# Cosine attention and a gated feed-forward layer on one core: the hand-written opening order replaced by another one

## Chip, cores, metric

One NeuronCore of a Trainium2 chip runs the kernel. The metric is the device time of one execution in microseconds (us). The engines are TensorE (PE, with its weight loads as PEld), VectorE (DVE), ScalarE (ACT), GpSimd (POOL) and SyncE (SP), which only issues DMAs here.

## What is computed

```
# q, k, v: (8 batches, 12 heads, 448 positions, 64); tau = 0.1
q_n = q / (norm(q, axis=-1) + 1e-6);  k_n = k / (norm(k, axis=-1) + 1e-6)
attn = softmax(q_n @ k_n.T / tau)                  # over 448 keys
x = (attn @ v) with heads side by side             # (3584, 768)
h = x @ w_in                                       # w_in (768, 2048)
out = (h * clip(h + 3, 0, 6) / 6) @ w_out          # w_out (2048, 768), float32
```

## The kernel before

**Work.** The heads are taken two at a time, 48 pairs in all and six to a batch. An "item" j is the q or the k of two pairs (448 KB); items 2d and 2d+1 belong to pairs 2d and 2d+1. When the six pairs of a batch are done, the batch's x stands transposed in `xT`, and the feed-forward layer runs on it in "units": 16 units of the first matrix product per batch (`mm1_unit`, line 589: six matmuls of 448 columns, line 598), and units of the second product, most of them by a fast two-by-two scheme with sums of weight blocks and of g blocks (`product_unit`, line 794, eight matmuls of 384 columns; `mm2_unit`, line 659, 16 of them). The first unit of batch 1 is the 17th.

**Order.** Nothing is reordered by a scheduler (`tc.manual_schedule()`): each engine runs its instructions in program order and waits on semaphores. The program has two parts. `PLAN` is a list of strings; each word is a step that `run` and `do` execute, so that PLAN writes out the order of everything from the first load to the turn of pair 17. After it a loop over pairs 18 to 47 places the same steps by rule, one pair a turn, with the feed-forward units of `TURNS` in between. All DMAs of inputs and outputs and all transposing DMAs are issued by SP, one after another, and weights by POOL.

The words, with the engine where it is fixed (otherwise a letter says it: a ScalarE, v VectorE, p POOL) and the line of the profile:

- `LQ.j` loads item j (SP, line 198), `LV.d` the v of two pairs (SP, four DMAs, line 212), `W` the next weight piece (POOL, line 1004; cast to bf16 on the way).
- `SQ.j.e.c.n` squares n of the columns of item j (lines 227 and 229), `RE.j` sums the squares over the head size (VectorE, line 241; `RE.j.h` one half). `NO.d` makes the reciprocal norms of two items with four ScalarE instructions (lines 257 to 260); `NA.d` (lines 272, 273) and `ND.d` (lines 284, 285) do the same with two on ScalarE and two on VectorE. `NM.j` multiplies (line 297; with a last number, one half).
- `TR.j` transposes item j on PE (line 342), or `XD.j` by a transposing DMA (SP, line 353). `CQ`, `CK`, `CS` copy the result to where the scores read it (lines 362, 364, 392, 402).
- `SC.i.g` are the scores of pair i, group g (PE, line 445), `EX.i.g` their exponentials (ScalarE, line 463), `VA.i.g` the products with v (PE, line 486), `FI.i` the division by the row sums (VectorE, lines 506, 507), `VC.i` the cast of v.
- `BK` and `CX` transpose a pair's result on PE and copy it into `xT`; `XP` and `XB` do it by DMA (lines 550, 538).
- `U` issues the next feed-forward unit on PE, `UA`, `UV` and `UP` the oldest open step on its results on ScalarE (relu, line 614), VectorE (product, line 620, which frees the PSUM bank) and POOL. `WS` sums weight blocks, `GS` blocks of g. `WS.y3` and `WS.y4` write over blocks of w_out that `mm2_unit` reads, so they follow units 31 and 32.
- `D.n` and `DP.n` are matmuls of zeros that keep PE busy while it has nothing to do (512 columns, line 1011; 248 columns, line 1016).

Until `OPEN`, scores go to two double PSUM buffers; after it, six single banks are handed out in a fixed ring (`next_bank`), to scores, units and transposes alike, and PE waits until the bank's last reader is done.

The weights: `w_in` comes in four pieces, two halves of its columns by two halves of its rows, and `w_out` in four pieces of four of its 16 row blocks; an assertion in `mm1_unit` holds that the pieces that a unit reads were issued:

```
assert len(weights) <= 6 - 2 * (2 * fc // FCN)
```

Of the kernel before, what the change touches and what calls it, by code (L numbers as in the profile page):

```python
# [18 lines left out]
ORDER = "1111111111111111111111111111112222222122"  # L19

PLAN = [
# [39 lines left out]
]  # L61


# [1 line left out]
def kernel(  # L65
# [11 lines left out]
    B, H, S, D = q.shape  # L77
    d_model, d_ff = moe_w_in.shape
# [5 lines left out]
    FCN = d_ff // 128  # L84
# [6 lines left out]
    w_in_r = moe_w_in.tensor.rearrange("(g n p) f -> g p n f", g=2, p=64)  # L91
# [10 lines left out]
    w_in_sb = const.tile([128, CC, d_ff], BF16, name="w_in_sb", tag="w_in_sb")  # L102
# [65 lines left out]
    def needs(*what):  # L168
        for w in what:
            assert w in issued or any(x < 0 for x in w[1:] if isinstance(x, int)), w  # L170
# [399 lines left out]
    def g_of(b):  # L570
        if b == B - 1:
            needs(("NM", NP - 1), ("RE", NP - 1), ("VC", NP - 1))
            return g_last
        return gT[b % 2]
# [15 lines left out]

    def mm1_unit(b, fc, ends=None):
        needs(*(("CX", i) for i in range(b * HP, (b + 1) * HP)))
        assert len(weights) <= 6 - 2 * (2 * fc // FCN)
        x, g, c0 = xT[b % 2], g_of(b), b % 2 * SR
        ps, key = bank_of(None, 1)
        def products_of(ccs):
# [83 lines left out]
    def firsts(b, *fcs):  # L680
        return [(mm1_unit, b, fc) for fc in fcs]
# [301 lines left out]
    f = firsts(b, *range(FCN))  # L983
# [3 lines left out]
    for n, x in enumerate("2176"):  # L987
# [4 lines left out]
    units[NP] += [(product_unit, n, x, 2) for n, x in ((10, "7"), (10, "6"), (11, "6"))]  # L992
    units[NP] += [(product_unit, 11, "7", x) for x in range(2)]

    FG = d_ff // 2
    weights = [
        (w_in_sb[64 * g : 64 * g + 64, :, f * FG : (f + 1) * FG], w_in_r[g, :, :, f * FG : (f + 1) * FG])
        for f in range(2)
        for g in range(2)
    ] + [(w_out_sb[:, 4 * f : 4 * f + 4, :], w_out_r[:, 4 * f : 4 * f + 4, :]) for f in range(4)]  # L1000

# [76 lines left out]
    SC = [psum_s.tile([128, 2, 512], FP32, name=f"SC{n}", tag=f"SC{n}") for n in range(2)]  # L1078
# [114 lines left out]
```

## Time and profile before

| | |
|---|---|
| three runs | 404.18, 404.43, 405.69 us; median 404.43 |
| the profiled execution | 402.04 us, of which the span of the program's instructions is 399.5 |
| busy, share of the span | PE 98%, VectorE 72%, ScalarE 68%, POOL 61%, weight loads 58% |
| granted TensorE clock | 1.00 in the profiled execution |
| chain that ended last | PE 90%, ScalarE 3%, VectorE 3%, POOL 2%, DMA 1% |

A row of a timeline gives start, duration, engine, source line, operation and tiles; of engines that overlap two instructions, the duration runs past the next one's start, and the distance of two starts is what an instruction costs in a full queue. The chain of waits is followed back from the last instruction, at each step to what released it. Sums by stretch give the busy time and the number of instructions of each engine between two moments.

### The profile page before, as it was taken

To read this page: it belongs to the slowest core of one execution; us is meant where nothing else is said; L and a number is where in the kernel's file an instruction comes from. 1 tells how busy PE (TensorE), PEld (TensorE's weight loads), DVE (VectorE), ACT (ScalarE), POOL (GpSimd) and SP (SyncE) were. 2 spreads that over 40 slices of the span, in tenths; PEclk is the share of its full clock that TensorE was granted. 3 is DMA by queue.
4 is the path that set the end of the run, shared out by engine and by line. 5 is a ranking of instruction groups with operands and counts; after the bars stand their busy time and mean duration, and the time that the engine had idled before them with its cause. 6 is when DMAs were issued, how large, how long until landed. Compare 5 with 4: busy or idle time off the path is not lost.

```text
span 399.5 us, 9630 instructions
## 1 busy us (share of the span) xinstructions
PE 391.9 (98%) x3677; PEld 231.6 (58%) x3677; DVE 289.5 (72%) x513; ACT 271.9 (68%) x624; POOL 242.6 (61%) x236
## 2 busy tenths in 40 slices
PE   7999999999999999999999999999999999999996
PEld 4666555555665556555555555555565556555564
DVE  6897689899877598776778775886766565645663
ACT  6899988776977676887776776767658655224230
POOL 7899556392654999389859829688395500400070
PEclk9999999999999999999999999999999999999999
DMA  8999977999988677795778397895853424230133
GB/s 292 299 229 260 235 186 147 243 165 211 175 175 187 157 203 176 177 229 154 188 187 225 79 184 183 169 180 142 187 131 70 102 48 67 46 74 21 30 71 97
DMA packets 91565, 63.73 MB, mean 160 GB/s; under 512 B 56064, under 2 KB 89984, under 8 KB 91520
## 3 DMA queue, kind: packets, MB, share of 16 engines
q1 hardware_dynamic: 87408, 56.45, 59.7%
q0 software_dynamic: 3712, 6.29, 9.1%
q8 instruction: 28, 0.46, 0.5%
q10 hardware_dynamic: 400, 0.39, 0.3%
q14 instruction: 17, 0.14, 0.1%
HBM read 45.61 MB, written 11.01 MB: 142 GB/s over the span
## 4 chain that ended last, share of the span: by engine, by line
PE 90%; ACT 3%; DVE 3%; POOL 2%; DMA 1%; issue 1%; SPq 0%; POOLq 0%; ACTq 0%
PE M L598 23%; PE M L794 18%; PE PV L486 11%; PE Y L598 6%; PE M L445 6%; PE Z L598 5%; PE Z L794 5%; PE Y L794 4%; PE PV L1016 3%; ACT at L463 2%; PE M L874 1%; PE Z L445 1%; PE Y L445 1%; DMA tT<-nrm 1%; PE SC L445 1%; PE M L659 1%
## 5 line engine op out<-in xcount | busy, mean ns | idle before, releaser
L598 PEld LDWEIGHTS <-w_in_sb 128*128 128x128 bf16 x768 | 72.1, 98 | 63.0 <-issue 2.5
L463 ACT ACTIVATE at<-M 128x448 bf16<-128x448 f32 x199 | 99.4, 574 | 13.5 <-PE M L445 12.0
L598 PE MATMUL M<-xT,w_in_sb 128*128 128x448 bf16 x510 | 107.8, 353 | 0.0
L297 POOL TENSOR_TENSOR nrm<-big,r 128x896 bf16<-128x896 f32 (+1 forms) x47 | 79.0, 1685 | 25.9 <-ACT at L463 9.5
L229 POOL TENSOR_TENSOR big<-big 128x896 f32<-128x896 f32 (+3 forms) x42 | 65.1, 1555 | 14.2 <-DVE n L241 8.7
L614 ACT ACTIVATE u<-M 128x448 bf16<-128x448 f32 x85 | 47.9, 565 | 31.0 <-PE M L598 30.0
L486 PEld LDWEIGHTS <-at 128*128 128x128 bf16 (+1 forms) x1536 | 53.8, 97 | 22.9 <-issue 13.7
L620 DVE SCALAR_TENSOR_TENSOR gT<-u,M 128x448 bf16<-128x448 bf16 x74 | 45.2, 617 | 28.5 <-ACT u L614 28.4
L486 PE MATMUL PV<-vx,at 128*128 128x65 bf16 (+1 forms) x1536 | 63.2, 193 | 0.2 <-DVE on L507 0.2
L241 DVE TENSOR_REDUCE n<-big 128x14 f32<-128x896 f32 (+1 forms) x50 | 51.8, 1041 | 5.8 <-POOL big L229 4.8
L794 PEld LDWEIGHTS <-gT 128*128 128x128 bf16 x336 | 32.5, 98 | 23.5 <-DVE gT L772 0.7
L823 POOL TENSOR_TENSOR big<-big 128x384 f32<-128x384 f32 x13 | 13.4, 1033 | 53.7 <-ACT big L842 53.5
L794 PE MATMUL M<-w_out_sb,gT 128*128 128x384 bf16 x216 | 39.0, 326 | 0.3 <-DVE gT L772 0.3
L794 PEld LDWEIGHTS <-gs 128*128 128x128 bf16 x280 | 27.0, 98 | 18.7 <-issue 0.6
L402 POOL COPY km<-tT 64x128 bf16<-64x128 bf16 x34 | 12.6, 372 | 38.1 <-DMA tT<-nrm 20.5
L507 DVE TENSOR_TENSOR on<-PV,rc 128x512 bf16<-128x512 f32 x48 | 33.2, 692 | 1.7
L794 PE MATMUL M<-w_sum,gs 128*128 128x384 bf16 (+1 forms) x192 | 34.1, 323 | 0.1
L445 PE MATMUL M<-tT,kz 64*128 64x448 bf16 (+1 forms) x177 | 31.9, 351 | 0.1
L463 ACT ACTIVATE at<-Y 128x448 bf16<-128x448 f32 x47 | 27.0, 574 | 6.1 <-PE Z L445 5.9
L598 PE MATMUL Z<-xT,w_in_sb 128*128 128x448 bf16 x132 | 28.7, 353 | 0.0
L463 ACT ACTIVATE at<-Z 128x448 bf16<-128x448 f32 x48 | 27.6, 575 | 1.2 <-PE Z L445 0.8
L598 PE MATMUL Y<-xT,w_in_sb 128*128 128x448 bf16 x126 | 27.3, 353 | 0.0
(140 smaller groups left out, 560.1 us busy)
## 6 DMA issues: line engine op xcount, KB each, us to landing
big<-in_k_dram SPq DMA_DIRECT2D x24, 448.0 KB, 4.4
big<-in_q_dram SPq DMA_DIRECT2D x24, 448.0 KB, 4.2
out_dram<-o SPq DMA_DIRECT2D x107, 96.0 KB, 2.2
big<-in_v_dram SPq DMA_DIRECT2D x48, 128.0 KB, 4.1
big<-in_v_dram SPq DMA_DIRECT2D x48, 96.0 KB, 4.0
w_in_sb<-in_moe_w_in_dram POOLq DMA_DIRECT2D x4, 768.0 KB, 11.4
w_out_sb<-in_moe_w_out_dram POOLq DMA_DIRECT2D x4, 768.0 KB, 8.7
tT<-nrm SPq DMA_TRANSPOSE x34, 2.8
```

Source lines behind the costliest of these rows:

```text
L229: engines[e].tensor_tensor(out=o, in0=i, in1=i, op=ALU.mult)
L241: nc.vector.tensor_reduce(out=n2s[d % 2][:, j % 2, c], in_=sq[:, :, :, :].rearrange("p g c d -> p (g c) d")[:, c, :], axis=AX.X, op=ALU.add,)
L297: engines[e].tensor_tensor(out=nrm[:, :, g, :].rearrange("p c g d -> p g c d"), in0=raw_of[j][:, g, :, :], in1=rs[d % 2][3][:, j % 2, :] . ...
L445: nc.tensor.matmul(o, ks, qt[rows], start=True, stop=True)
L463: nc.scalar.activation(out=o, in_=x, func=AF.Exp, scale=inv_tau)
L486: nc.tensor.matmul(pv_out(j, h), at[rows, n, q_cols(i // HP, j)], vt[rows, 3 + h if name == "M" else 5 * h + int(name[1]), :], start=(name ...
L507: nc.vector.tensor_tensor(out=on[:, :, :, :].rearrange("p j h d -> p h j d"), in0=pv4[:, :, :, 0:D], in1=rc[:, :, :].to_broadcast([128, 2, ...
L598: nc.tensor.matmul(ps[:, 0:S], w_in_sb[:, cc, fc * 128 : (fc + 1) * 128], x[:, cc, 0:S], start=(cc == 0), stop=(cc == CC - 1),)
L614: nc.scalar.activation(out=u[:, :], in_=ps[:, 0:S], func=AF.Relu, bias=0.5, scale=1.0 / 6.0)
L620: nc.vector.scalar_tensor_tensor(out=g[:, fc, c0 : c0 + S], in0=u[:, :], scalar=1.0, in1=ps[:, 0:S], op0=ALU.min, op1=ALU.mult,)
L794: nc.tensor.matmul(m, lhs[:, c, :], rhs[:, c, c0 : c0 + width], start=(base is None and c == 0), stop=(c == KC - 1), skip_group_check=True,)
L823: nc.gpsimd.tensor_tensor(out=e, in0=d, in1=e, op=ALU.add)
```

## The change

PLAN is replaced by another order of the same work. What differs beside the order:

- Fill: 92 matmuls instead of 93, with `D.10` first of all.
- The first two items are squared whole on ScalarE; before, ScalarE, POOL and VectorE shared them. Over the plan ScalarE squares 16 times (before 13, some of them parts), POOL 10 (17), VectorE 3 (4).
- Six `NA`/`ND` and six `NO` (before one and eleven).
- `NM` on VectorE for items 2, 5, 7 and 19 (before 2, 12 and 18).
- Copies: `CK` on ScalarE four times (one), `CQ` three (one), `CX` four (two), `CS` once (three times). `VC` on POOL 13 times (nine), on ScalarE two (three), on VectorE five (eight).
- `W` ten times (eight): the first half of the columns of `w_in` in quarters. Five pieces are issued before the first unit (before two).
- `WS.7.p.0` alone is on POOL; before, `WS.6.p.0` too.
- `LV.11` stands before `XP.14` and `NO.10` before `SQ.22`; before, after them.

```diff
-    "LQ.1 DP.5 SQ.1.a.11.3 SQ.1.p.4.3 DP.1 SQ.1.a.0.4 LQ.0 SQ.0.p.8.6 DP.2 DP.4 LQ.3 LQ.2 SQ.1.v.7.4 RE.1.1",
-    "SQ.0.a.0.6 RE.1.0 NO.0.1 LQ.5 LQ.4 SQ.0.v.6.2 DP.6 SQ.3.a.0.7 NM.1.p.0 D.10 RE.0.1 DP.3 NM.1.p.1 RE.0.0 DP.8",
-    "NO.0.0 LV.0 DP.2 SQ.2.a.0.7 NM.0.p.0 RE.3 RE.2 NM.0.p.1 TR.1.Y DP.2 TR.0.Z CK.0.v DP.4 SQ.4.p.0.7 CQ.0.v",
-    "SQ.5.a.0.7 LQ.6 NO.1 LV.1 LQ.7 SC.0.0.0 SC.0.1.1 DP.5 DP.3 CQ.1.v EX.0.0 RE.5 RE.4 NM.3.p SC.0.2.0 CK.1.v",
...
-    "EX.7.0 LQ.13 SC.7.1 SC.7.2 FI.5 TR.9 SC.7.3 EX.7.1 VA.6.0 BK.5 EX.7.2 CK.9.v CK.8.v VA.6.1 CX.5.v CS.9.a",
-    "VA.6.2 EX.7.3 U LQ.15 SC.8.0 UA CS.8.v VC.8.a SC.8.1 EX.8.0 U VA.6.3.h UV SC.8.2 U VC.9.v EX.8.1 W SC.8.3",
...
-    "VA.16.2 VA.16.3.h SC.17.2 SC.17.3 FI.16 EX.17.1 XP.14 LV.11 U UA U U XB.16 UV UV EX.17.2 UV EX.17.3 SQ.22.a.0.7",
-    "VA.17.0 CS.18.v NO.10 CK.19.v VC.19.v NM.20.p RE.22 VC.18.p",
+    "D.10 LQ.1 DP.7 DP.5 LQ.0 SQ.1.a.0.14 DP.8 SQ.0.a.0.14 RE.1.1 LQ.3 DP.4 RE.1.0 LQ.2 NA.0.1 RE.0.0 ND.0.1",
+    "NM.1.p.1 NM.1.p.0 SQ.3.a.0.7 RE.0.1 DP.5 NO.0.0 LQ.5 SQ.2.a.0.7 NM.0.p.0 TR.1.Y DP.8 NM.0.p.1 DP.10 TR.0.Z",
+    "RE.3 LQ.4 CK.0.v CK.1.v RE.2 CQ.0.v NO.1 SQ.5.p.0.7 LV.0 SQ.4.a.0.7 DP.8 LQ.6 SC.0.0.0 EX.0.0 SC.0.1.1",
+    "EX.0.1 CQ.1.v DP.5 DP.4 NM.3.p SC.0.2.0 TR.3.Y RE.5 VC.0.v EX.0.2 RE.4 LV.1 VA.0.0 LQ.8 SC.0.3.1 DP.3 NM.2.v",
+    "SC.1.0.0 NA.2 CK.2.v TR.2.Z LQ.7 EX.0.3 ND.2 SC.1.1.1 EX.1.0 LV.2 NM.5.v DP.9 VC.1.v SC.1.2.0 CQ.2.v CQ.3.v",
...
+    "CX.4.v EX.7.1 VA.6.0 VA.6.1 LQ.12 SQ.10.p.0.7 BK.5 EX.7.2 TR.9 RE.10 CX.5.a CS.8.v SC.7.3 U CK.8.a CS.9.a",
+    "SQ.11.p.0.7 SC.8.0 U EX.7.3 UA SQ.12.p.0.7 CK.9.a LV.4 EX.8.0 VA.6.2 UA LQ.13 VA.6.3.h RE.11 SC.8.1 UV",
...
+    "EX.14.2 VA.14.0 VA.14.1 UA SC.14.3 GS.-1.5 SC.15.0 GS.-1.2 EX.14.3 NM.18.p UV U SQ.20.a.0.7 UA WS.y3.v.0",
+    "LV.8 WS.6.v.1 VC.15.a VA.14.2 WS.1.v.1 U WS.y3.v.1 WS.y4.v.0 XP.12 U EX.15.0 SC.15.1 WS.7.v.1 UV UA",
+    "WS.y4.v.1 EX.15.1 SC.15.2 RE.20 SC.15.3 CK.16.v U EX.15.2 NM.19.v LQ.21 CK.17.v UA GS.-1.1 EX.15.3 CS.16.v",
...
+    "XP.14 U UA UV U EX.17.2 XB.16 U NO.10 UV EX.17.3 UV SQ.22.a.0.7 VA.17.0 CS.18.v VC.18.v RE.22 NM.20.p",
...
-        assert len(weights) <= 6 - 2 * (2 * fc // FCN)
+        assert len(weights) <= 8 - 2 * min(2, 4 * fc // FCN)
...
-    FG = d_ff // 2
+    PIECES = [slice(0, d_ff // 4), slice(d_ff // 4, d_ff // 2), slice(d_ff // 2, d_ff)]
     weights = [
-        (w_in_sb[64 * g : 64 * g + 64, :, f * FG : (f + 1) * FG], w_in_r[g, :, :, f * FG : (f + 1) * FG])
-        for f in range(2)
+        (w_in_sb[64 * g : 64 * g + 64, :, f], w_in_r[g, :, :, f])
+        for f in PIECES
         for g in range(2)
     ] + [(w_out_sb[:, 4 * f : 4 * f + 4, :], w_out_r[:, 4 * f : 4 * f + 4, :]) for f in range(4)]
```

The lines of the changed kernel stand one lower from the PLAN on (line 598 is 597 there).

58 rows, old and new, of the table PLAN are left out of this document.

## The prediction

> **What bounds the kernel now.** I read the page's busy shares, then the sums by stretch, the chain of waits in order of time, and each engine's timeline. Times are from the span's start (399.5 us). The first exponential starts at 12.14, the first feed-forward unit (six matmuls of line 598) at 41.11, the last instruction of the plan at 113.3.
>
> ```profile
> core 0: us, PE busy (x) PEld busy (x) DVE busy (x) ACT busy (x) POOL busy (x), PEclk, DMA share, GB/s
> 0.00:12.10 12.10, 9.56 (x65) 6.40 (x65) 8.54 (x31) 7.62 (x19) 9.50 (x24) 1.00 0.88 287
> 12.10:41.10 29.00, 28.44 (x403) 18.69 (x402) 24.48 (x53) 27.65 (x55) 27.32 (x23) 1.00 1.06 266
> 41.10:113.30 72.20, 72.16 (x717) 41.30 (x715) 61.04 (x110) 60.02 (x140) 40.16 (x37) 1.00 0.93 193
> 113.30:137.00 23.70, 23.12 (x232) 13.50 (x230) 17.54 (x28) 16.80 (x42) 16.22 (x15) 1.00 0.73 162
> 137.00:399.50 262.50, 258.59 (x2269) 151.73 (x2267) 177.87 (x293) 159.81 (x371) 149.43 (x140) 1.00 0.58 133
> ```
>
> PE's busy time overlaps itself, so I count its work by spacing: 0.189 us for each 448 columns, 0.162 for 384, 0.029 for 65 (starts of neighbours in a run). From 12.1 to 41.1 that gives 16.6 us of real work, from 41.1 to 113.3 it gives 67.6 of 72.2, from 113.3 to 137 it gives 21.6 of 23.7, after that 251.4 of 262.5. So PE sets the end from 41 on and loses 4.6 and 2.1 us in the two stretches that the change can reach. Before 41 it waits: ScalarE is busy for 27.65 of 29.0 us there, VectorE for 24.48. The clock is full throughout. The chain confirms both readings:
>
> ```profile
> 30.08 1.35 ACT at L463 x2
> 31.45 2.98 ACT at L463 x4
> ...
> 41.11 1.14 PE M L598 x6
> ...
> 121.07 1.08 DVE n L241
> 122.16 0.07 SPq L538
> 122.22 0.05 issue
> 122.28 0.58 SPq L198
> 122.85 0.05 issue
> 122.91 0.02 SPq L353
> 122.92 0.03 issue
> 122.95 4.33 DMA tT<-nrm
> ```
>
> The exponentials carry the start. In the loop's first turns (after 113.3) the chain leaves PE for SP's queue and a transposing DMA. SP's timeline says why:
>
> ```profile
> 111.72 1.55 SPq L550 DMA_TRANSPOSE xT<-on  x1
> 113.38 2.68 SPq L212 DMA_DIRECT2D big<-in_v_dram  x4
> 116.15 1.22 SPq L538 DMA_TRANSPOSE xT<-on  x1
> 117.47 3.43 SPq L647 DMA_DIRECT2D out_dram<-o  x4
> 121.00 1.23 SPq L538 DMA_TRANSPOSE xT<-on  x1
> ```
>
> Each row starts where the one before it ends: SP is a line of issues, and LV.11 (line 212) stands ahead of all that the loop needs.
>
> **The change, part by part.** The reordered loop after the plan is untouched; the program's work is the same but for two more weight DMAs, one matmul of fill less, five pairs of root operations (NA on ScalarE, ND on VectorE) in place of NO, and steps that change engine. Costs are start-to-start spacings of before's rows: exponential of two banks 0.80, of one 0.43; square on ScalarE 0.84, on POOL 1.64; sum RE 1.0; NO 0.99, NA 0.47, ND 0.57; normalise 1.65 on POOL, 1.0 on VectorE; FI 0.85; relu 0.43, product 0.53; weight sum 0.9.
>
> *To the first exponential.* Before, three engines share the squares and EX.0.0 starts at 12.14. After, LQ.1 and LQ.0 land at 4.20 and 5.41 as before (same issues). ScalarE squares them by 6.3; VectorE's four half sums end at 7.85; ND.0 ends at 7.3, so POOL's four half normalisations (0.9 each) run from 7.35 to 10.95; before, the last ended at 10.6. PE is the new wait: 29 small fill matmuls at 0.106 after the ten wide ones end at 9.7; TR.1 follows; behind it stand DP.8 and DP.10, 18 x 0.106 = 1.9 us, so TR.0 ends at 12.4; then eight more, and SC.0.0 at 13.25. ScalarE does SQ.4 in that hole. EX.0.0 at 13.65: **1.5 us late**.
>
> *From there to the first unit.* ScalarE's plan from EX.0.0 to EX.7.0 is 25.2 us before (28 exponentials of pairs 0 to 6, four NO, one square, one copy), and it took 26.5. After it is 22.7: of the four NO one stays, two become NA, one comes later, and CX.3 goes to VectorE (−2.97 + 0.94 − 0.41). VectorE's from EX.0.0 to the first unit rises from 24.6 to 25.7 (two normalisations, two ND, a CS and a CQ more; three CK, one RE and one VC fewer). POOL falls from 24.5 to 21.2. I followed the order by hand, each step starting at the latest of its engine's last step and its inputs: EX.1.0 at 17.3, EX.3.0 24.9, EX.4.0 27.7 (before 28.17), EX.5.0 31.0 (31.45), EX.6.0 34.4 (35.69; NO.5 and CX.3 stood ahead of it), EX.7.0 37.4 (38.67), CX.4 on VectorE 38.7, CX.5 on ScalarE 40.35, first unit's end 40.55 against 42.25. From the 1.7 us I take 0.25 for VA.6.2, now behind the unit, and 0.15 for waits I missed. **−1.3 us.** Bounds: −2.0 if ScalarE never waits, +1.5 if the late exponential stays late.
>
> *Weights.* Five pieces instead of two are issued before the first unit. POOL pays 0.70 each; it has 3.3 us less to do there. They leave POOL from 26.6 to 30.7; the slowest weight DMA of before took 13.2 us to land, so the quarters are there at 40. W6 (fc 8 and up) leaves near 43, its unit U9 runs at 56.8. Nothing. If quarters were as slow as halves and queued, still nothing until U5.
>
> *First to fortieth unit.* ScalarE's plan grows from 57.3 to 62.4 us, VectorE's falls from 63.7 to 62.4, POOL's from 45.8 to 44.0, and PE has 72. Followed the same way, with six PSUM banks handed out in order: ahead of before by 1.2 at U9 (work done included), 1.3 at U13, 1.2 at U21, 1.1 at U31. The extra ScalarE work (2.7 us of squares, three CK, two CQ, two CX) lies beside PE. Then VectorE has WS.y3.v.0, WS.6.v.1, WS.1.v.1, WS.y3.v.1, WS.y4.v.0, WS.7.v.1 in a row ahead of the copy that frees U32's bank for SC.15.3: 6 x 0.87 = 5.2 us from 93.3 (when U31 has read its first half), so 98.5 plus 0.5; PE asks at 99.2. Covered, just; if y3 must wait for all of U31 (94.5), SC.15.3 and U34 are 1.2 us later. Lead at the plan's end 0.95: **+0.35 us**, bounds −1.0 and +3.0.
>
> The last weight piece, W10, now follows NM.16 and goes out near 82.6; before, it left at 83.16 and landed at 90.82. U31's matmul 12 is the first to read it, at 93.8. No wait.
>
> *Entry to the loop.* LV.11 moves ahead of XP.14 and NO.10 ahead of SQ.22, so SP reaches XD.20 2.7 us sooner (that row), and POOL's km copies, which waited 5.8 us, go sooner too. Of the 2.1 us that PE loses there I take a quarter, since two sums on VectorE (line 772, to 120.9) stand there as before: **−0.5 us**, between 0 and −2.1. Once the loop is PE's, nothing more is won or lost.
>
> *Sum:* −1.3 + 0.35 − 0.5 = −1.45. The profiled execution took 402.04 us (span and 2.5 around it), so 400.6 for it. The runs' median, 404.43, is 2.4 above that execution; I carry the difference over: **403.0 us**.
>
> **One rule against the change.** VectorE's two-input normalise at 60.88 lasted 1.09 us, and POOL's, begun at 61.00, took 2.52 in place of 1.69: one held the other up.
>
> ```profile
> 61.00 2.52 POOL L297 TENSOR_TENSOR nrm<-big,r 128x896 bf16<-128x896 f32 x1 [1.50 <-DVE r L285]
> ```
>
> The Trainium skill (SBUF — State Buffer, Who interferes with whom) says that a VectorE instruction with two SBUF inputs and a GpSimd one that reads SBUF exclude each other, and that whichever issues first makes the other block fully. This row agrees with it. By that rule the sum stays as it is if NM.4 on POOL is the one held, and rises by at most POOL's 1.65 if NM.5 on VectorE is, both being released by ND.2.
>
> **Rivals.**
>
> *1. The waits at the loop's entry go altogether.* XD.20 lands by 123 and not 127.3, and the chain 121–134 (DMA, km copies, POOL's sums, line 851) dissolves: −1.3 + 0.35 − 2.1 = −3.0, **401.4 us**. For it: 17 us of that chain hang on one DMA. Against it: VectorE's 772 rows and ScalarE's fuller tail.
>
> *2. VectorE becomes the bound: slower.* Before, it executed 24.6 us of steps in 28.6, 4 idle. After, it begins its stretch at 12.75, and 24.3 us of steps lead to CX.4. My walk leaves it 1.65 idle. With 4 idle CX.4 ends at 41.05; if NM.5, released together with POOL's NM.4, is held for POOL's 1.65 as well (the row of line 297 above shows such a hold the other way round), at 42.7, and the first unit ends near 44, 1.7 late. Its row of weight sums then costs its 1.2: +1.7 − 0.25 + 0.35 + 1.2 = +3.0, **407.4 us**. It decides from about 3 us of VectorE idle time between 12.75 and CX.4. For it: VectorE was busy for 24.48 of 29.0 and gets more. Against it: half of its idle time before was waiting for exponentials that now come sooner.
>
> That the order is not what the text says is excluded: the instruction lists of both kernels show it.
>
> **How the numbers follow.** Forecast (403.0; its own range 402.4 to 404.4) 0.43, rival 1 0.32, rival 2 0.22, another way 0.03. A measurement of this kernel tells about 0.5% (2.0 us) from no change. Faster by over that: rival 1 and a little, 0.34; within: 0.43; slower: 0.23. The range reaches to rival 1 with its bound (−2.0 for the start) and most of rival 2: 400.0 to 406.8.
>
> **What would show it.** Right: EX.0.0 near 13.7 and EX.7.0 near 37.4; the first unit's end near 40.6; U31 (line 659) starting near 91.9 with VA.14 and SC.15.0 done; plan's end near 112.4; XD.20's issue before 120. Wrong: a first unit after 42; ScalarE waiting over 3 us between 14 and 37; SC.15 or line 794 waiting for VectorE's line 738; a wait of line 598 or 659 for weights.

## The result, and the profile after

The changed kernel takes 408.48 us (median of 6 runs, 406.80 to 409.56), the kernel before in the same comparison 404.31 (402.34 to 405.69): a ratio of 1.0116, 95% interval 1.0083 to 1.0150, so 3.4 to 6.1 us slower (the two medians alone would give 1.0103). Forecast were 403.0 us and no difference that a measurement can tell.

The profiled execution of the changed kernel took 409.56 us with a span of 406.8. Sums by stretch, cut at the first exponential (13.6), the first feed-forward unit (41.2), the end of the fortieth unit (119.3) and, as far behind it as before, at 143.0:

```profile
core 0: us, PE busy (x) PEld busy (x) DVE busy (x) ACT busy (x) POOL busy (x), PEclk, DMA share, GB/s
0.00:13.60 13.60, 11.12 (x84) 7.56 (x85) 8.40 (x32) 7.81 (x17) 8.83 (x23) 1.00 0.90 290
13.60:41.20 27.60, 25.13 (x372) 16.42 (x371) 25.44 (x54) 25.55 (x48) 22.66 (x20) 1.00 0.99 253
41.20:119.30 78.10, 75.71 (x729) 42.48 (x728) 61.73 (x113) 63.67 (x150) 39.00 (x39) 0.98 0.89 176
119.30:143.00 23.70, 22.00 (x215) 13.08 (x214) 16.65 (x28) 16.63 (x39) 14.25 (x13) 1.00 0.77 160
143.00:406.80 263.80, 259.60 (x2288) 152.16 (x2284) 177.99 (x294) 159.71 (x371) 149.69 (x141) 1.00 0.58 134
```

The first unit starts about where it did (41.21, before 40.95). In the stretch from there to the plan's end, which took 72.2 us before and takes 78.1, PE has gaps, and the clock's mean is 0.98. By starts of units: U1 to U40 (line 793) 76.78 us, before 71.06; U40 to the eighth unit behind it 14.13 and 14.10; from there to the end 274.6 and 273.4, a part in which the plan has no say and which took 273.4 to 275.5 in the profiles of the kernel before and of its variants. So the loss sits between U1 and U40. It is 5.7 us in these two executions, which lie further apart than the medians do; by the ratio the whole loss is some 4.7 us.

More than half of it is one place. VectorE's timeline, then POOL's, then PE's (the last column is the idle time before a row and what ended it):

```profile
85.72 4.50 DVE L737 TENSOR_TENSOR w_sum<-w_out_sb 128x1536 bf16<-128x1536 bf16 x1
90.14 0.61 DVE L619 SCALAR_TENSOR_TENSOR gT<-u,M 128x448 bf16<-128x448 bf16 x1
```

```profile
85.47 0.80 POOL L1003 DMA_DIRECT2D w_out_sb<-in_moe_w_out_dram  x1
86.30 3.10 POOL L737 TENSOR_TENSOR w_sum<-w_out_sb 128x1536 bf16<-128x1536 bf16 x1
```

```profile
88.30 0.36 PE L444 MATMUL M<-tT,kz 64*128 64x448 bf16 x1
90.80 0.35 PE L444 MATMUL M<-tT,kz 64*128 64x448 bf16 x1 [2.14 <-DVE gT L619]
91.08 2.17 PE L597 MATMUL M<-xT,w_in_sb 128*128 128x448 bf16 x6
```

The weight sum WS.1.v.0 takes 4.50 us; its like takes 0.95. It ends 0.82 us after POOL's sum WS.7.p.0 (89.40). In the order before, it stood ahead of POOL's two sums. VectorE, then POOL:

```profile
83.22 0.95 DVE L738 TENSOR_TENSOR w_sum<-w_out_sb 128x1536 bf16<-128x1536 bf16 x1
```

```profile
86.38 6.16 POOL L738 TENSOR_TENSOR w_sum<-w_out_sb 128x1536 bf16<-128x1536 bf16 x2
```

In the changed kernel the products behind WS.1.v.0 free PSUM banks late, and PE stands idle for 2.14 us. Then the six matmuls of U28 take 1.97 us, start to start, in place of 1.14. Sums by microsecond say why (the granted clock stands third from the end):

```profile
89.00:90.00 1.00, 0.00 (x0) 0.00 (x0) 1.00 (x1) 0.00 (x0) 0.40 (x1) 1.00 1.49 62
...
91.00:92.00 1.00, 1.00 (x5) 0.44 (x5) 1.00 (x2) 1.00 (x3) 0.00 (x0) 0.69 1.17 216
92.00:93.00 1.00, 1.00 (x4) 0.38 (x3) 1.00 (x3) 0.26 (x1) 0.00 (x0) 0.50 1.11 235
...
94.00:95.00 1.00, 1.00 (x14) 0.69 (x12) 1.00 (x3) 0.57 (x3) 0.00 (x0) 0.60 1.13 319
```

The start holds the same thing in small. VectorE, then POOL, at the two normalisations that ND.2 releases together:

```profile
17.04 0.33 DVE L284 RECIPROCAL r<-le 128x28 f32<-128x28 f32 x1
17.46 2.62 DVE L296 TENSOR_TENSOR nrm<-big,r 128x896 bf16<-128x896 f32 x1
```

```profile
17.45 1.69 POOL L296 TENSOR_TENSOR nrm<-big,r 128x896 bf16<-128x896 f32 x1 [2.78 <-DVE r L284]
19.08 1.47 POOL L315 CAST vx<-big 128x512 bf16<-128x512 f32 x1
```

NM.5 on VectorE stands until NM.4 on POOL is done and then takes its 1.0; POOL's next step, VC.3, stands until NM.5 is done. Such a step, which stands at the head of its queue until the other engine's operation is done, is called held below.

Where a loss is summed up below, PE's lost time is the time that its useful matmuls, counted at full clock, do not fill.

### The profile page after: what moved, and what is told of

It reads as the page before. It is cut to its first block, busy times and chain, and to the rows that moved or that the text cites. A ratio compares the mean times of both kernels' runs of the same rounds, so it can differ in the third digit from the quotient of the medians.

```text
span 406.8 us, 9610 instructions
## 1 busy us (share of the span) xinstructions
PE 393.6 (97%) x3676; PEld 231.7 (57%) x3676; DVE 290.2 (71%) x518; ACT 273.4 (67%) x619; POOL 234.4 (58%) x233
## 4 chain that ended last, share of the span: by engine, by line
PE 77%; DMA 8%; DVE 6%; ACT 3%; POOL 2%; issue 2%; SPq 1%; DVEq 0%; POOLq 0%; ACTq 0%
PE M L597 21%; PE M L793 17%; PE PV L485 9%; PE Y L597 6%; DMA big<-in_v_dram 5%; PE Z L793 4%; PE Y L793 4%; PE Z L597 4%; PE M L444 4%; DMA tT<-nrm 2%; ACT at L462 1%; PE M L658 1%; PE M L873 1%; PE PV L1015 1%; PE Z L444 1%
## 5 line engine op out<-in xcount | busy, mean ns | idle before, releaser
L597 PE MATMUL M<-xT,w_in_sb 128*128 128x448 bf16 x516 | 110.6, 355 | 0.2 <-DMA xT<-on 0.2
L597 PEld LDWEIGHTS <-w_in_sb 128*128 128x128 bf16 x768 | 72.2, 98 | 65.8 <-issue 6.4
L462 ACT ACTIVATE at<-M 128x448 bf16<-128x448 f32 x193 | 96.7, 568 | 15.4 <-PE M L444 13.0
L296 POOL TENSOR_TENSOR nrm<-big,r 128x896 bf16<-128x896 f32 (+1 forms) x46 | 75.9, 1655 | 33.6 <-DVE r L284 16.5
L485 PEld LDWEIGHTS <-at 128*128 128x128 bf16 (+1 forms) x1536 | 53.9, 97 | 24.3 <-issue 14.9
L228 POOL TENSOR_TENSOR big<-big 128x896 f32<-128x896 f32 (+1 forms) x35 | 58.9, 1686 | 7.6 <-ACT at L462 3.1
L462 ACT ACTIVATE at<-Y 128x448 bf16<-128x448 f32 x49 | 27.9, 569 | 6.3 <-PE Z L444 6.2
L462 ACT ACTIVATE at<-Z 128x448 bf16<-128x448 f32 x52 | 29.5, 567 | 0.4 <-PE M L444 0.4
L597 PE MATMUL Y<-xT,w_in_sb 128*128 128x448 bf16 x132 | 28.7, 354 | 0.0
L315 POOL CAST vx<-big 128x512 bf16<-128x512 f32 x41 | 27.6, 678 | 0.1
```

The costliest lines, as they stand in the source:

```text
L228: engines[e].tensor_tensor(out=o, in0=i, in1=i, op=ALU.mult)
L296: engines[e].tensor_tensor(out=nrm[:, :, g, :].rearrange("p c g d -> p g c d"), in0=raw_of[j][:, g, :, :], in1=rs[d % 2][3][:, j % 2, :] . ...
L315: (engines[e].copy if e == "a" else engines[e].tensor_copy)(out=o, in_=f)
L462: nc.scalar.activation(out=o, in_=x, func=AF.Exp, scale=inv_tau)
L485: nc.tensor.matmul(pv_out(j, h), at[rows, n, q_cols(i // HP, j)], vt[rows, 3 + h if name == "M" else 5 * h + int(name[1]), :], start=(name ...
L597: nc.tensor.matmul(ps[:, 0:S], w_in_sb[:, cc, fc * 128 : (fc + 1) * 128], x[:, cc, 0:S], start=(cc == 0), stop=(cc == CC - 1),)
```

## The experiments

Theory A: VectorE's and POOL's operations with two inputs in SBUF (the engines' on-chip memory, other than PSUM) shut each other out, and two such holds, at steps that were not held before, cost the time. The kernel before was timed beside each run again, at 402.9 to 403.8 us, so ratios are compared. Rivals: VectorE is too full, so that any step moved only moves the wait; weights that land late; ScalarE's squares.

**e1, NM.5 later.**

```diff
-    ... EX.1.0 LV.2 NM.5.v DP.9 VC.1.v SC.1.2.0 CQ.2.v CQ.3.v
+    ... EX.1.0 LV.2 DP.9 VC.1.v SC.1.2.0 CQ.2.v CQ.3.v NM.5.v
```

> The changed kernel with one step moved on VectorE: the normalisation NM.5 stands behind VC.1, CQ.2 and CQ.3 and not ahead of them, so that it no longer starts in the same moment as NM.4 on POOL (17.46 and 17.45 us, both released by ND.2; NM.5 took 2.62 us in place of 1.0). Theory A, the two engines exclude each other and the start-up lost 1.2 us by this one hold: NM.5 takes 1.1 us at most 1.3, the gap of 0.83 us ahead of EX.2.0 on ScalarE goes, EX.7.0 starts near 37.4 (38.62 in the changed kernel), the first unit near 40.0 (41.21), and the time falls by 1.2 us, to about 407.3. Rival R, VectorE is simply too full there: the steps behind NM.5 come sooner but others later; EX.7.0 stays after 38.3 and the time within 0.4 us of 408.5.

407.10 us, ratio 1.0089 (1.0060 to 1.0119). VectorE's timeline:

```profile
19.18 1.66 DVE L296 TENSOR_TENSOR nrm<-big,r 128x896 bf16<-128x896 f32 x1
```

Still 0.66 held (NM.4 ran from 18.21 to 19.90), but behind the copies that mattered. This execution began 0.8 later (EX.0.0 at 14.36), so distances count: from EX.0.0 to EX.7.0 23.83 us, 25.03 in the changed kernel, and 25.0 to 25.2 in every other run that left NM.5 and the start's order in place. The hold costs 1.2 us at the first unit. Theory A holds here; the time fell by 0.27%, 1.1 us, though the intervals overlap.

**e2, WS.1.v.0 later**, behind WS.6.v.0.

```diff
-    EX.13.3 CS.14.v UV UA WS.1.v.0 LV.9 ...
+    EX.13.3 CS.14.v UV UA LV.9 ...
-    ... NO.9 U UV W WS.6.v.0 VA.13.3.h
+    ... NO.9 U UV W WS.6.v.0 WS.1.v.0 VA.13.3.h
```

> The changed kernel with one step moved on VectorE: the weight sum WS.1.v.0 (85.72 us, 4.50 us long in place of 0.95) stands behind WS.6.v.0, some 4.6 us of VectorE's work later, when POOL's WS.7.p.0 (86.30 to 89.40) is over. Theory A, POOL's two-input sum held it, the relus and banks behind it held PE idle from 88.66 to 90.80, and the granted clock then was 0.5 to 0.7 until 95: no sum on VectorE above 1.2 us, no PE gap over 0.5 us and a clock of 1.00 between 80 and 100, U31 (line 658) at about 93.3 in place of 98.63, time down by 4.5 to 5.5 us, to about 403.5. Rival W, the sum waited for its weight piece or for W10's issue on POOL beside it: the same 3.5 us show up at the piece's readers or at the next step beside W10's issue, and U31 stays after 96.5. Rival R, VectorE is too full: U31 comes 1 us sooner at most, time above 407.

406.62 us, 1.0079 (1.0051 to 1.0108). Less than expected: the sum met POOL again. VectorE, POOL, PE:

```profile
92.07 3.31 DVE L737 TENSOR_TENSOR w_sum<-w_out_sb 128x1536 bf16<-128x1536 bf16 x2
```

```profile
92.73 1.83 POOL L296 TENSOR_TENSOR nrm<-big,r 128x896 bf16<-128x896 f32 x1 [2.44 <-ACT r L259]
```

```profile
96.28 0.65 PE L485 MATMUL PV<-vx,at 128*128 128x65 bf16 x16 [1.76 <-DVE on L506]
```

NM.18 waits for WS.6.v.0 and then holds WS.1.v.0 (which takes 2.44 of the 3.31 us, in place of 0.95); FI.13 behind it is late, and PE waits 1.76. U31 comes 9.42 us behind U27 (11.56 in the changed kernel, 6.14 before). Its own expected figure failed, the mechanism did not.

**e3, the roots of items 10 and 11 sooner.**

```diff
-    ... CK.9.a LV.4 EX.8.0 VA.6.2 UA LQ.13 VA.6.3.h RE.11 SC.8.1 UV",
-    ... RE.12 NA.5 SC.8.3 EX.8.2 U VA.7.0 UA SC.9.0 ND.5 U
+    ... CK.9.a LV.4 RE.11 NA.5 EX.8.0 VA.6.2 UA LQ.13 VA.6.3.h SC.8.1 UV ND.5",
+    ... RE.12 SC.8.3 EX.8.2 U VA.7.0 UA SC.9.0 U
```

> The changed kernel with the roots of items 10 and 11 sooner: NA.5 on ScalarE ahead of EX.8.0 and ND.5 on VectorE behind the first UV (and RE.11 ahead of NA.5 in the text, in its old place on VectorE). Theory A, the late reciprocals (48.2 us) make POOL idle for 2.14 us ahead of NM.10, and NM.10, NM.11, TR.11 and the sixth unit follow one another (52.08 for U6, 49.76 before the change): NM.10 starts near 46.1, U6 near 50.0, U27 1.2 to 2 us sooner than 87.07, time down by about 1.5 us, to about 407.0. Rival V, the sixth unit waits for the v items (LV.4 lands from 44.4 to 49.48, beside the weight pieces) and POOL's casts of them: U6 stays after 51.5 and the time within 0.4 us of 408.5. Rival R, ScalarE is full there (9.07 of 10 us): U6 comes sooner but U9 stays after 59, time within 0.5 us.

408.73 us, 1.0138 (1.0108 to 1.0168): nothing won. NM.10 started at 46.51 as expected (48.28), yet U6 came 10.75 us behind U1 (10.87). What sets that stretch stays open, since the run brought two delays of its own. At U1 the chain of waits goes back to a weight piece:

```profile
29.33 12.34 DMA w_in_sb<-in_moe_w_in_dram
41.66 0.14 issue
41.80 1.31 PE M L597 x6
```

And a tiny VectorE step of ND.5, 0.17 us elsewhere, was held beside POOL's square from 44.32 to 46.02:

```profile
44.46 1.60 DVE L283 TENSOR_SCALAR le<-nr 128x28 f32<-128x28 f32 x1
```

The chain of waits up to U6 runs through this step, so that the 1.4 us of this hold take back part of what NM.10 won. No step waits for v items there, so rival V is not what set it.

**e4, the three moves together.**

> The changed kernel with all three moves at once (NM.5 later, WS.1.v.0 later, NA.5 and ND.5 sooner). Theory A: the three losses add, 1.2 + 5 + 1.5, so about 400.8 us, 3.5 us below the kernel before; first unit near 40.0, U6 near 48.8, U27 near 84.3, U31 near 90.5. Rival R, full engines: what is won at one place is waited for at the next, time above 405.

406.20 us, 1.0077 (1.0042 to 1.0113). EX.0.0 came at 14.59 in the profile. The losses did not add: WS.1.v.0 was held by NM.18 as in e2, and U6 came 11.47 us behind U1.

**e5, WS.1.v.0 ahead of RE.19**, between POOL's two operations.

```diff
-    EX.13.3 CS.14.v UV UA WS.1.v.0 LV.9 ...
-    VA.13.1 XD.16 UA RE.19 ...
+    EX.13.3 CS.14.v UV UA LV.9 ...
+    VA.13.1 XD.16 UA WS.1.v.0 RE.19 ...
```

> The changed kernel with WS.1.v.0 once more at another place of VectorE: ahead of RE.19, so behind POOL's WS.7.p.0 and ahead of its NM.18. Behind WS.6.v.0 it had met NM.18 (92.73) and taken 2.44 us. Theory A, a two-input operation of VectorE that is issued while POOL runs one waits for POOL's end: here POOL is idle, so WS.1.v.0 takes 0.95 us, no VectorE row of lines 737 and 771 between 84 and 98 takes over 1.2, PE loses 1.0 us or less between 85 and 100 (4.9 in the changed kernel, 2.75 with WS.1.v.0 behind WS.6.v.0), U31 comes 7.5 us behind U27 (11.56 and 9.42 there), and the time is 1.5 us below that of that run, about 405.0. Rival R, VectorE is full there (8.9 of 10 us busy) and PE waits wherever the sum stands: U31 stays over 9 us behind U27, time 406 or more.

404.68 us, 1.0039 (1.0014 to 1.0064): 0.77% below the changed kernel, the intervals apart. The sum takes 0.95, the clock stays at 1.00, PE loses 1.2 us between 85 and 100 (before 0.8, changed 4.9), U31 comes 7.93 us behind U27. (Some 1.1 to 1.3 us of the distance to 6.14 is work: 24 more products with v and three more scores stand between these units in the new order.) One step moved by 4 us wins two thirds of the loss; a full VectorE does not explain that.

**e6, WS.7 from POOL to VectorE.**

```diff
-    VA.13.1 XD.16 UA RE.19 ... UA WS.7.p.0 FI.13
+    VA.13.1 XD.16 UA WS.7.v.0 RE.19 ... UA FI.13
```

> The changed kernel with the sum WS.7.p.0 taken from POOL and given to VectorE ahead of RE.19; WS.1.v.0 stays at its place, beside W10's issue on POOL (85.47 to 86.27 in the changed kernel). It tells what held WS.1.v.0 for 3.5 us. Theory A1, POOL's sum alone: WS.1.v.0 takes 0.95. Theory A2, the writing of W10's descriptors held it first, and POOL's sum took over: it takes 1.3 to 1.5 us. Rival W, it waited for a weight piece (W9 landed at 88.60): it still takes over 4 us. Under A1 and A2 VectorE has one sum more (0.9), PE does not go idle between 88 and 91, U31 comes some 7.5 to 8.5 us behind U27 (11.56), and the time is about 405.0.

405.42 us, 1.0049 (1.0019 to 1.0078). VectorE and POOL:

```profile
86.44 0.95 DVE L737 TENSOR_TENSOR w_sum<-w_out_sb 128x1536 bf16<-128x1536 bf16 x1
```

```profile
86.19 0.80 POOL L1003 DMA_DIRECT2D w_out_sb<-in_moe_w_out_dram  x1
```

WS.1.v.0 stands where it stood, beside W10's issue, and takes 0.95 us; W9 landed at 89.60. So neither W10's descriptors nor a weight piece held it: POOL's sum did.

**e7, less fill.** 17 fill matmuls out.

```diff
-    "D.10 LQ.1 DP.7 DP.5 LQ.0 ...
+    "D.10 LQ.1 DP.5 LQ.0 ...
-    ... TR.1.Y DP.8 NM.0.p.1 DP.10 TR.0.Z",
+    ... TR.1.Y DP.8 NM.0.p.1 TR.0.Z",
```

> The changed kernel with 17 of the small fill matmuls taken out ahead of the first transposes: 22 in place of 29 ahead of TR.1, 8 in place of 18 between TR.1 and TR.0; the squares stay whole on ScalarE. Theory F, the first exponential is late because PE is still at its fill when the first items are ready (normalised at 9.36 and 11.15 us; the transposes start at 9.46 to 10.46 and 11.76 to 12.76 in the profiles so far): TR.1 near 9.4, TR.0 near 11.2, EX.0.0 near 13.0 (13.48 to 14.59 so far), time down by 0.6 to 1.5 us, to 407.0 to 407.9. Rival S, the whole squares on ScalarE set it (the normalisations of item 0 end at 11.15, before the change at 10.6): EX.0.0 after 13.3, time unchanged. Rival K, PE goes idle and its clock drops: matmuls of 0.2 us and more between 9 and 14, EX.0.0 later than 13.5.

406.75 us, 1.0076 (1.0037 to 1.0114). PE and ScalarE:

```profile
9.46 0.56 PE L341 MATMUL Y<-ident,nrm 128*128 128x128 bf16 x7 [0.94 <-POOL nrm L296]
...
11.24 0.56 PE L341 MATMUL Z<-ident,nrm 128*128 128x128 bf16 x7 [0.38 <-POOL nrm L296]
```

```profile
11.85 0.23 ACT L256 ACTIVATE ln<-n 128x28 f32<-128x28 f32 x1 [2.06 <-DVE n L240]
```

The transposes now wait for the norms, not for the fill. EX.0.0 stays at 13.60, because NO.1 and SQ.4 stand ahead of it on ScalarE and wait for RE.2, which stands behind CK.0 and CK.1 on VectorE. Less fill could thus only help in executions in which the fill ends late; that it does is not shown. With the full fill EX.0.0 came between 13.47 and 14.86 in twelve profiles; the first 39 fill matmuls were over at 9.46 in the changed kernel and at 10.46 in e4. In the three profiles of the kernel before and of its variants it came at 12.04 to 12.15.

**e8, a hold put into the kernel before.**

```diff
-    ... U CS.14.v WS.1.v.0 UV UV LV.9
-    ... EX.13.3 U UV UA LV.8
+    ... U CS.14.v UV UV LV.9
+    ... EX.13.3 U UV WS.1.v.0 UA LV.8
```

> The kernel before, with one step moved on VectorE: WS.1.v.0, which started at 83.22 us as a POOL operation ended and took 0.95, stands behind the product that follows CK.15 (86.95), so that it is issued while POOL runs its two sums WS.6.p.0 and WS.7.p.0 (86.38 to 92.53). Nothing else differs. Theory A, POOL's running two-input operation holds VectorE's: it takes 3.4 us (until 89.43 and 0.9 more) or, if POOL's second sum follows without letting VectorE in, 6.4; PE goes idle behind it and its granted clock falls below 1.00 between 88 and 98; the time rises by 3 us in the first case, 5 to 8 in the second. Rival R, place does not matter: 0.95 to 1.2 us and the time within 0.7 us of that before.

403.32 us, 1.0000 (0.9975 to 1.0025). It did not produce the case: WS.1.v.0 started at 86.34, 0.15 us ahead of POOL's sum, and POOL's was the one held.

```profile
86.34 0.95 DVE L738 TENSOR_TENSOR w_sum<-w_out_sb 128x1536 bf16<-128x1536 bf16 x1
...
91.85 3.14 DVE L738 TENSOR_TENSOR w_sum<-w_out_sb 128x1536 bf16<-128x1536 bf16 x2
```

```profile
86.49 6.82 POOL L738 TENSOR_TENSOR w_sum<-w_out_sb 128x1536 bf16<-128x1536 bf16 x2
```

POOL has slack there and loses 0.66 us without a loss of time. The hold that this pushes onto WS.1.v.1 (1.3 us) is covered as well. So a hold costs what stands behind it: on the engine that PE waits for, microseconds; elsewhere, nothing that the time shows. Whether a hold on VectorE would slow the kernel before was not tried again.

**e9, quarters alone in the kernel before** (`PIECES` and the assertion as in the change, each of the first two `W` twice).

> The kernel before with one part of the change alone: the first half of the columns of w_in in quarters, four pieces in place of two at the two old places in POOL's row. Theory N, as the prediction had it: the pieces cost POOL 0.7 us each beside idle time and nothing else, time within 0.5 us of that before. Rival Q, the smaller packets land later and hold the loads behind them: the first unit's second piece, which landed at 40.80 for a unit at 40.95, lands after 42, the first unit waits for it, time 0.7 to 1.5 us up.

403.66 us, 0.9985 (0.9961 to 1.0010): no difference. The first unit's second piece landed at 31.57. The quarters are not what costs.

**e10, the mends so far** (e1, e5, e7, `RE.2` ahead of `CK.0.v`, and the first two `W` ahead of `SQ.9.p.0.7`).

> The changed kernel with all that the runs so far point to: NM.5 behind CQ.3, WS.1.v.0 ahead of RE.19, 17 fill matmuls less ahead of the first transposes, RE.2 ahead of CK.0 and CK.1 on VectorE (so that NO.1 and SQ.4 no longer stand late ahead of EX.0.0), and the first two weight pieces on POOL ahead of SQ.9 (24.3 in place of 28.3 us, since the second has landed at 36.0 to 41.7 for a first unit at 41). If the losses are those two holds and the start: EX.0.0 near 13.1, EX.7.0 near 36.6, first unit near 39.5 without a wait for weights, U31 7.5 to 8 us behind U27, time 402.0, below that before by 1.5 to 2. Rival R, full engines give the rest back: 404 or more.

404.48 us, 1.0019 (0.9996 to 1.0041). EX.0.0 came at 13.24. The two early `W` pushed NM.6 back, and the exponentials of pair 5 came 4.26 us behind those of pair 4 (3.23 in the changed kernel; e15's expectation counts the same delay from a neighbouring row), so the start's gain was gone. And PE met a new wait:

```profile
94.92 2.12 PE L658 MATMUL M<-w_out_sb,gT 128*128 128x384 bf16 x12
98.61 0.81 PE L658 MATMUL M<-w_out_sb,gT 128*128 128x384 bf16 x4 [1.57 <-DMA w_out_sb<-in_moe_w_out_dram]
```

With U31 early, W10 (issued at 85.39, landed at 98.57) is late for its thirteenth matmul.

**e11, PE kept busy through the hold.**

```diff
-    ... RE.18 UV SC.14.0 U UA VA.13.0
+    ... RE.18 UV DP.18 SC.14.0 U UA VA.13.0
```

> The changed kernel with 18 small fill matmuls on PE ahead of SC.14.0, into the 2.1 us in which PE stood idle behind the held WS.1.v.0; the hold stays. It separates the hold from the clock that fell behind it (0.50 to 0.69 from 91 to 95 us). Theory C, the idle time lowered the clock and that cost some 2 us beside the hold itself: WS.1.v.0 still takes over 4 us, the clock stays at 1.00, U28 starts within 0.3 us of 91.08, and U31 at 96.5 to 97.0 in place of 98.63; time 1.5 to 2 us down, about 406.7. Rival D, the low clock is only a mark of waiting: U31 and the time stay.

408.20 us, 1.0098 (1.0071 to 1.0125). WS.1.v.0 took 4.49, U28 came 4.01 us behind U27 as in the changed kernel, and:

```profile
91.00:92.00 1.00, 0.98 (x8) 0.49 (x6) 1.00 (x2) 0.00 (x0) 0.00 (x0) 1.00 3.60 42
92.00:93.00 1.00, 0.78 (x4) 0.31 (x4) 1.00 (x3) 0.74 (x2) 0.00 (x0) 1.00 2.04 32
```

The clock stayed at 1.00. That the fill kept it there is not shown, for in e1 (and e3) it stayed at 1.00 without fill, behind the same hold of 4.50 us and the same 2.14 us of idle PE:

```profile
90.37 0.35 PE L444 MATMUL M<-tT,kz 64*128 64x448 bf16 x1 [2.14 <-DVE gT L619]
```

```profile
91.00:92.00 1.00, 1.00 (x13) 0.59 (x11) 1.00 (x2) 0.83 (x3) 0.00 (x0) 1.00 1.35 67
```

In the changed kernel and in e7 it fell to 0.5 for 3.41 us behind that gap. So the gap is followed by a fall of the clock in some executions and not in others. On what a fall costs, all five agree: U31 comes 11.56 and 11.49 us behind U27 with it, and 10.66 without it (e1, e3, e11). That is 0.9 less, half of what was expected: VectorE's row behind the sum is full and sets the pace then. Of the 3.6 us that e5 won at U31, the clock was 0.9 and the hold 2.7. The time did not tell 0.9 us from nothing.

**e12, the loop's entry as before.**

```diff
-    "LV.11 VA.16.0 UP UV ...
-    "XP.14 U UA UV U EX.17.2 XB.16 U NO.10 UV EX.17.3 UV SQ.22.a.0.7 ...
+    "VA.16.0 UP UV ...
+    "XP.14 LV.11 U UA UV U EX.17.2 XB.16 U UV EX.17.3 UV SQ.22.a.0.7 NO.10 ...
```

> The changed kernel with the loop's entry as before: LV.11 behind XP.14 and NO.10 behind SQ.22. Theory P, the prediction's: LV.11 ahead of XP.14 lets SP reach XD.20 sooner, so that undoing it costs 0.5 us or more, up to 2.7 on XD.20. Rival S, SP's row has no gap in either order (from 101.95 to 130 each issue starts as the one before ends), XD.20 stands behind both, and nothing changes: XD.20 within 0.4 us of its distance from U40 (11.9 us), time within 0.5 us of 408.5.

409.33 us, 1.0121 (1.0091 to 1.0152): no difference. SP's timelines, the changed kernel and e12:

```profile
119.21 2.67 SPq L211 DMA_DIRECT2D big<-in_v_dram  x4
121.97 1.27 SPq L549 DMA_TRANSPOSE xT<-on  x1
...
129.86 2.71 SPq L352 DMA_TRANSPOSE tT<-nrm  x2
```

```profile
119.23 1.57 SPq L549 DMA_TRANSPOSE xT<-on  x1
120.86 2.67 SPq L211 DMA_DIRECT2D big<-in_v_dram  x4
...
129.84 2.63 SPq L352 DMA_TRANSPOSE tT<-nrm  x2
```

LV.11 and XP.14 change places and XD.20 starts at the same moment, though PE was 3.2 us later at U40 in e12. By accident this execution told more: W8 landed at 87.00, so both sums waited for it, VectorE went first, and POOL was held. VectorE and POOL, then the chain of waits:

```profile
87.09 0.96 DVE L737 TENSOR_TENSOR w_sum<-w_out_sb 128x1536 bf16<-128x1536 bf16 x1 [0.53 <-DMA w_out_sb<-in_moe_w_out_dram]
```

```profile
87.15 3.86 POOL L737 TENSOR_TENSOR w_sum<-w_out_sb 128x1536 bf16<-128x1536 bf16 x1
```

```profile
86.23 14.86 DMA w_out_sb<-in_moe_w_out_dram
101.09 0.04 issue
101.13 1.44 PE M L658 x4
```

No hold, and then U31 waited for W10 until 101.13. Which of the two delays an execution shows depends on a landing.

**e13, W10 sooner**, behind W9; **e14**, the same with e5's move.

```diff
-    "UA GS.-1.6 UV FI.12 W NM.17.p ...
-    ... VA.13.2 NO.9 U UV W WS.6.v.0 ...
+    "UA GS.-1.6 UV FI.12 W W NM.17.p ...
+    ... VA.13.2 NO.9 U UV WS.6.v.0 ...
```

> The changed kernel with the last weight piece W10 issued right behind W9 on POOL, ahead of NM.17 (near 78 us in place of 85.5). WS.1.v.0 stays where it is. Theory A, the port: POOL's WS.7.p.0 now follows NM.16 at 85.5, VectorE's sum, asked for at 85.8, is held until 88.6 and ends near 89.5 (90.22 in the changed kernel): U31 comes 0.8 us sooner, time down by 0.5 to 1. Theory P, the late piece is the loss: W10 lands near 91 and the time falls by 2 us or more.

407.80 us, 1.0138 (1.0113 to 1.0164): the piece alone is not the loss. VectorE and POOL show the hold, shorter as forecast, since POOL's sum started sooner:

```profile
86.06 3.67 DVE L737 TENSOR_TENSOR w_sum<-w_out_sb 128x1536 bf16<-128x1536 bf16 x1
```

```profile
85.83 3.08 POOL L737 TENSOR_TENSOR w_sum<-w_out_sb 128x1536 bf16<-128x1536 bf16 x1
```

> The changed kernel with W10 issued behind W9 and WS.1.v.0 ahead of RE.19. Against the run with WS.1.v.0 moved alone (404.68 us, its executions from 403.7 to 407.2). Theory A with the piece as the next wait: no execution waits at U31, the executions lie closer together (within 2 us), median 0.5 to 1 us lower, near 404.0; W10 lands by 92. Rival: three pieces in flight at once make W8, which WS.1.v.0 and WS.7.p.0 read, land after 88, the sums wait for it, and the median is not below 404.7.

404.69 us, 1.0067 (1.0048 to 1.0086), by the ratio no better than e5 (1.0039; the intervals overlap). W10 landed at 92.13 and nothing waited for it, yet the time shows no gain over e5: the piece's lateness is an occasional wait, not the regular loss.

**e15, all mends** (e10 with the first two `W` ahead of `SQ.8.p.0.7` and W10 behind W9); **e16, only e1, e5 and W10 behind W9.**

> The changed kernel with NM.5 behind CQ.3, WS.1.v.0 ahead of RE.19, W10 behind W9, 17 fill matmuls less, RE.2 ahead of CK.0, and the first two weight pieces ahead of SQ.8 on POOL (ahead of SQ.9 they had pushed NM.6 back: the fifth pair's exponentials came 4.4 us behind the fourth's in place of 3.4). If the losses add: EX.0.0 near 13.2, EX.7.0 near 37.0, first unit near 39.8, U31 7.6 us behind U27 with no wait for weights; time 402.0, that is 1.5 us or so below the kernel before. Rival R, full engines and the shared DMA engines give the start back: 403.7 or more.

> The changed kernel with the three moves that answer to one loss each: NM.5 behind CQ.3 (1.2 us at the first unit), WS.1.v.0 ahead of RE.19 (3.5 to 4) and W10 behind W9 (the wait that shows up next). If they add, 403.0 us, 0.7 below the kernel before; if the start's 1.2 us are lost again to the first unit's weight piece (landed at 36.0 to 41.7), 404.0.

e15 403.77 us, 1.0030 (1.0010 to 1.0050); e16 403.64, 1.0032 (1.0014 to 1.0049). Three moved steps take back all but 0.3% of 1.16%, though the third, W10, showed no gain of its own in e14. In e16 the first unit starts at 40.06 and U31 7.92 us behind U27; in e15 the early pieces again delayed pair 5 (4.25 us), U1 at 40.83. Neither beats the kernel before, and nothing that the runs showed points to a version that would.

What is left, 1.3 us in e16, lies spread: PE's lost time is 0.4 us below before at 40 us, 0.6 above at 60, 0.7 at 85, 1.1 at 100 and 1.8 at 150. The largest part falls between 40 and 60 us, where PE loses 2.97 us in the changed kernel, in e15 and in e16 alike, and 1.92 before. ScalarE, with more squares in the new order, is busy for 18.95 of these 20 us in e16 (18.49 before). No run moved the squares, so this rival stays open; no single wait carries the rest, and no run settled it.

## Why the prediction was wrong

- **To the first exponential: the number was right, the wait only half.** Forecast 13.65, measured 13.59. The fill was named as the wait, but with 17 of its matmuls less (e7) ScalarE's NO.1 and SQ.4 hold EX.0.0 until the same moment, 13.60: two waits end together. That the fill's own time varies by a microsecond, and that EX.0.0 comes at 13.9 to 14.9 in seven of twelve profiles, was not foreseen.
- **To the first unit: the walk was right but for one hold.** The walk gave EX.7.0 at 37.4; it came at 38.62, and with NM.5's hold avoided (e16) at 37.48. First unit's end 40.55 forecast, 42.34 measured, 41.19 in e16. The step that failed is the one under "One rule against the change": the sum was left as it is, "if NM.4 on POOL is the one held". NM.5 was, for 1.62 us, and 1.2 of them reached the first unit. The alternative stood beside it ("at most POOL's 1.65 if NM.5 on VectorE is"), and the sum took the other. The rule itself, the Trainium skill's (SBUF — State Buffer, Who interferes with whom), agrees with both rows.
- **Weights: "Nothing" and "No wait" held in the changed kernel only because its units came late.** The quarters as such cost nothing (e9). But the five pieces took 8.8 to 18.8 us to land, where 13.2 was taken as the slowest, and the four quarters were there at 46.84, not at 40. The first unit's second piece landed at 40.41, after the 39.4 at which the forecast had that unit start, and between 36.0 and 41.7 in the other runs that left its place alone. W10 went out at 85.47, not near 82.6, and landed at 95.02, after the 93.8 at which U31 was to read it; in the other runs with that place it landed at 93.8 to 101.1. A unit on time would have waited, as U1 did in e3 and U31 in e10 and e12.
- **First to fortieth unit: this is the step that failed.** Forecast +0.35 with bounds of −1 and +3, measured +5.7. The walk gave every instruction its usual duration and listed VectorE's weight sums from y3 on; WS.1.v.0 and POOL's WS.7.p.0, both in the same stretch, were never laid side by side. The one rule that was weighed was weighed at one place. The hold and the clock behind it are worth 3.6 us at U31 (e5); the row from y3 on, which the text feared, cost little: PE lost 0.4 us between 100 and 110. The walk was also some 1.0 us short between 40 and 60 us, in every version with the new order that was summed up; why stays open.
- **Entry to the loop: −0.5 forecast, 0.0 measured.** LV.11 was moved inside a row of issues with no gap in it: a transfer put first only swaps places with the next, and everything behind both comes when it came (e12). The prediction had said so itself, "Each row starts where the one before it ends", and the sum still took a gain. The plan's end was late too: XD.20 went out at 129.86, not before 120. And the rule applied on this very stretch, unread: in the profile before, one of VectorE's two sums of line 772, at 119.09, took 2.06 us in place of 0.68 beside POOL's normalisation of 118.47.
- **Rival 2 was the nearest**: 407.4 us with NM.5's hold as its mechanism and the weight sums as a follower. Its hold was right in kind, place and length. Its price at the first unit's end was not (1.7 late, measured 0.1), and the larger part of the loss came from the other hold, so that its total came within 1.1 us of the measured one by luck. Its point of decision, VectorE's idle time, was not the one that decided: from 13.6 to 41.2 it was 2.2 us, less than the 3 it asked for.

## What to carry to other kernels

When a step moves, or changes engine, lay VectorE's and POOL's two-input operations of the stretch side by side on the clock, all of them, before giving each its usual duration: such a pair cost the engine that came second up to the length of the other's operation and a little more (3.55 us here beside POOL's sum of 3.10). Put the pair so that the engine with slack is the one held. In a queue without gaps, count the order only for what stands between the two places of the moved step, and when a stretch gets faster, look up the next landing: a margin that was ample becomes the bound.

## What the runs showed of the hardware

- The start of the rows does not always tell who is held. VectorE's sum was in its queue's front at 85.81, POOL's row starts at 86.30, and VectorE was held (so too in e1, e3, e7 and e11, with the two rows' starts 0.57 to 0.58 us apart); in e8 0.15 us and in e12 0.06 us of lead were enough for VectorE. In the first cases POOL came straight from issuing a DMA. The Trainium skill (SBUF — State Buffer, Who interferes with whom) says that issue order decides; by the rows' starts that fails here, and what counts as POOL's issue in that case was not tried.
- A one-input VectorE step of 28 columns took 1.60 us in place of 0.17 beside a POOL operation (e3). The same section of the skill names `tensor_scalar` among those that can take the shared ports; the row agrees. It also infers that a two-input sum takes only the read side while descriptors need the write side: in e6 the sum beside a weight DMA's issue took its 0.95, which agrees.
- Behind 2.14 us of idle PE the granted clock fell to 0.5 for 3.41 us in the changed kernel and in e7, and stayed at 1.00 in e1 and e3. The Trainium skill (TensorE: Matmul & The Clock Gate, What's actually happening) speaks of one idle window of about 3.4 us; the stretch at 0.5 is as long as that, but the gap ahead of it was shorter.
- The last weight piece, 768 KB, took 7.7 us to land in the kernel before and 8.2 to 14.9 in the variants of the changed one, where it went out 2.3 us later beside W9, which had left 3 us later as well.
